# Twelve matmuls on zeros ahead of the first picks, a limit on the loads under way, and a new order, in a kernel of capped attention and a top-128 feed-forward block

## The chip, the core and the metric

The kernel runs on one core of a Trainium2 chip. A core has the engines TensorE (PE, matmuls), VectorE (DVE), ScalarE (ACT), GpSimd (POOL) and SyncE (SP, whose queue issues most of the transfers). The time of a run is the device time in microseconds. The kernel before was run three times.

## The reference

The first part is attention over 8 batches, 12 heads, 448 rows and a head width of 64. Scores are capped by a tanh before the softmax. The second part takes the 768 columns of all heads of a batch as one row per token, scores each token with a gate vector, picks the 128 best tokens of each batch, sends them through a feed-forward block of 768 to 1024 to 768 columns and adds the gated result to those tokens.

```python
scores = scale * np.matmul(q, k.transpose(0, 1, 3, 2))
scores = cap * np.tanh(scores / cap)
...
attn = attn / (np.sum(attn, axis=-1, keepdims=True) + 1e-09)
return np.matmul(attn, v).astype(np.float32)
...
    top_idx = np.argpartition(-scores[b], capacity)[:capacity]
    xe = x[b, top_idx]
    h = np.maximum(xe @ w1, 0.0)
    ye = h @ w2
    g = 1.0 / (1.0 + np.exp(-scores[b, top_idx]))
    out[b, top_idx] = x[b, top_idx] + g[:, None] * ye
```

## The kernel before, in words

**Tiling.** Four heads of a batch make a Double, so that there are 24 of them, three to a batch. Their keys are cut into three blocks of 128 rows and one of 64. The scores of a block of four heads are one unit for ScalarE: a tanh and then an exp over 128x1792 numbers. The 64-row blocks of two Doubles share a unit, so two Doubles make seven units, and the whole has 84. Scores are made on TensorE from q and k as they are (L691, "quarter" form) or from their splits into a high and a low part (`qh`, `ql`, `kh`, `kl`, made on VectorE at L647 and L653; L681, "wide" form). The values matmuls (L706) multiply the exponentials p of a block with v and accumulate in `psV`. When all four blocks of a Double are in, VectorE evacuates `psV` in two halves (L737, L738, L743 each); there is one `psV`, so the first values matmul of the next Double waits for the second half. A values step is 56 matmuls in a row of the trace, and a score unit is 16 in quarter form or 12 in wide form.

**Banks.** In the first phase the scores use six banks (`psE`, tanh and exp at L1252 and L1261). From unit `SIX` on they use four (`psS`, L1298 and L1305), and the two freed banks (`psT`) serve the picks and the feed-forward block.

**Feed-forward.** After the third Double of a batch VectorE has the gate scores of all its tokens (L772, L799, L801), sends them once through memory so that they lie in a row (L810, L813), counts for each token how many stand above it (L842, L850), and makes a one-hot matrix `sel` from the ranks (L881). TensorE's eight small "pick" matmuls (L891) turn it into the 128 indices, VectorE rounds them (L900 to L905), GpSimd gathers the rows (L909), TensorE transposes them (L938), and the two layers follow as 512- and 384-column matmuls (L992). Weights are split into high and low parts (L567, L570) as they arrive.

**What sets the order.** Every engine's instructions are written by a planner at build time, by a simulated clock for each engine. On TensorE the order of scores (Q) and values (V) steps is given by a string, `SCRIPT`; a number behind a letter says how many feed-forward pieces may go ahead of that step. For the other engines each task has a priority, which the table `EARLIER` shifts. The written order is what each engine executes; each instruction then only waits for its operands. SP issues all loads of q, k, v (L620) and weights (L555) and the stores of the results (L758, L761) from one queue, in order. A load waits until the buffer that it overwrites has been read.

## Time and profile before

| | |
|---|---|
| median of 3 runs | 435.36 us (434.31, 435.36, 437.21) |
| profiled execution | 435.0 us |
| its span | 433.2 us |
| TensorE matmul busy | 418.9 us, 97% of the span |
| ScalarE busy | 305.4 us, 71% |
| VectorE busy | 279.0 us, 64% |
| GpSimd busy | 27.5 us, 6% |
| granted TensorE clock, mean | 0.999 |
| chain that ended last | TensorE 81%, DMA 5%, ScalarE 5%, VectorE 3% |

The span is the time from the first to the last instruction of the profiled execution; 1.8 us of the execution lie around it. A time row reads: start and duration in microseconds, engine, line, operation, output and inputs, their shapes, and how many instructions the row joins; in brackets at the end how long the engine had stood idle before it, and what ended that. Ends of matmuls overlap the next start a little, so differences of starts are the better measure of their cost.

### The profile page before, as it was taken

To read this page: it belongs to the slowest core of one execution; us is meant where nothing else is said; L and a number is where in the kernel's file an instruction comes from. 1 tells how busy PE (TensorE), PEld (TensorE's weight loads), DVE (VectorE), ACT (ScalarE), POOL (GpSimd) and SP (SyncE) were. 2 spreads that over 40 slices of the span, in tenths; PEclk is the share of its full clock that TensorE was granted. 3 is DMA by queue.
4 is the path that set the end of the run, shared out by engine and by line. 5 is a ranking of instruction groups with operands and counts; after the bars stand their busy time and mean duration, and the time that the engine had idled before them with its cause. 6 is when DMAs were issued, how large, how long until landed. Compare 5 with 4: busy or idle time off the path is not lost.

```text
span 433.2 us, 17857 instructions
## 1 busy us (share of the span) xinstructions
PE 418.9 (97%) x8080; PEld 353.9 (82%) x8080; DVE 279.0 (64%) x861; ACT 305.4 (71%) x197; POOL 27.5 (6%) x73
## 2 busy tenths in 40 slices
PE   8989998999999999999999999999999999999994
PEld 5546586888799889898799888988789898879894
DVE  1596988959664688558745876738947695168241
ACT  5999999797886588694697586879787698411000
POOL 2000010100100001010010100101000010000101
PEclk9999999999999999999999999999999999999999
DMA  7995557550551562462181370472371321220202
GB/s 253 402 396 183 174 171 247 180 184 12 186 186 47 147 217 61 138 229 70 41 291 42 109 258 4 123 245 80 101 242 47 106 92 45 72 70 2 74 3 78
DMA packets 33268, 60.73 MB, mean 140 GB/s; under 512 B 10304, under 2 KB 20288, under 8 KB 33184
## 3 DMA queue, kind: packets, MB, share of 16 engines
q1 hardware_dynamic: 31456, 52.72, 37.1%
q0 software_dynamic: 1440, 6.56, 4.8%
q8 instruction: 65, 1.06, 1.0%
q10 hardware_dynamic: 288, 0.23, 0.2%
q14 instruction: 19, 0.16, 0.1%
HBM read 45.33 MB, written 14.17 MB: 137 GB/s over the span
## 4 chain that ended last, share of the span: by engine, by line
PE 81%; DMA 5%; ACT 5%; DVE 3%; issue 3%; POOL 1%; SPq 0%; POOLq 0%; DVEq 0%; ACTq 0%
PE psV L706 30%; PE psT L992 22%; PE psS L681 15%; PE psB L992 4%; PE psS L691 3%; DMA vlent<-in_v 2%; PE psE L691 2%; PE psE L681 2%; ACT p L1252 2%; ACT p L1261 1%; PE psT L938 1%; DMA p<-out,idx 1%; PE psV L992 1%; ACT plent L1261 1%; ACT plent L1252 1%
## 5 line engine op out<-in xcount | busy, mean ns | idle before, releaser
L706 PEld LDWEIGHTS psV<-v,p 128*64 128x64 f32 (+1 forms) x3864 | 104.8, 137 | 21.4 <-issue 14.7
L706 PE MATMUL psV<-v,p 128*64 128x65 f32 (+1 forms) x3864 | 111.6, 222 | 4.5 <-issue 2.4
L1298 ACT ACTIVATE p<-psS,sc 128x1792 f32<-128x1792 f32 x48 | 84.1, 1753 | 39.0 <-PE psS L681 22.7
L1305 ACT ACTIVATE p<-p,capc 128x1792 f32<-128x1792 f32 x48 | 86.1, 1794 | 1.4
L681 PE MATMUL psS<-qh,kh 64*128 64x448 f32 x220 | 42.6, 384 | 0.0
L706 PEld LDWEIGHTS psV<-v,plent 128*64 128x64 f32 (+1 forms) x1288 | 34.9, 137 | 8.1 <-issue 3.2
L737 DVE RECIPROCAL rec<-psV 128x7 f32<-128x7 f32 x48 | 9.6, 199 | 49.3 <-PE psV L706 49.3
L1298 ACT ACTIVATE plent<-psS,sc 128x1792 f32<-128x1792 f32 x16 | 28.0, 1752 | 16.9 <-PE psS L681 8.1
L706 PE MATMUL psV<-v,plent 128*64 128x65 f32 (+1 forms) x1288 | 37.6, 222 | 2.0 <-POOL vlent L667 1.2
L772 DVE CUSTOM_DVE_ANT_0 jk<-xn,gates 128x256 bf16<-128x256 f32 x72 | 30.4, 422 | 1.5
L1305 ACT ACTIVATE plent<-plent,capc 128x1792 f32<-128x1792 f32 x16 | 28.7, 1793 | 0.5
L738 DVE TENSOR_TENSOR xn<-psV,rec 128x384 f32<-128x384 f32 x48 | 26.8, 558 | 1.7
L1261 ACT ACTIVATE p<-p,capc 128x1792 f32<-128x1792 f32 x14 | 25.1, 1792 | 0.5
L1252 ACT ACTIVATE p<-psE,sc 128x1792 f32<-128x1792 f32 x14 | 24.3, 1737 | 0.6 <-PE psE L681 0.6
L842 DVE TENSOR_SCALAR_CACHE_REDUCE jk<-row,score 128x512 bf16<-128x512 f32 (+1 forms) x32 | 23.7, 742 | 0.9
L681 PEld LDWEIGHTS psS<-qh,kh 64*128 64x128 f32 x220 | 20.7, 185 | 2.6 <-ACT p L1298 0.2
L647 DVE CAST kh<-k 128x896 fp32r<-128x896 f32 x20 | 12.5, 624 | 13.0 <-PE psS L681 11.0
L992 PE MATMUL psT<-w2l,hh 64*128 64x384 f32 x192 | 20.7, 336 | 0.0
L681 PE MATMUL psS<-qlent,kh 64*128 64x448 f32 x112 | 20.5, 362 | 0.0
L681 PE MATMUL psS<-qh,klent 64*128 64x448 f32 x112 | 20.5, 362 | 0.0
L992 PE MATMUL psT<-w2h,hh 64*128 64x384 f32 x192 | 20.2, 339 | 0.0
L691 PE MATMUL psE<-q,k 64*64 64x448 f32 x176 | 19.6, 548 | 0.4 <-ACT p L1252 0.4
(179 smaller groups left out, 686.0 us busy)
## 6 DMA issues: line engine op xcount, KB each, us to landing
v<-in_v SPq DMA_DIRECT2D x23, 455.0 KB, 4.7
q<-in_q SPq DMA_DIRECT2D x22, 448.0 KB, 5.5
k<-in_k SPq DMA_DIRECT2D x22, 448.0 KB, 6.1
out<-xn SPq DMA_DIRECT2D x24, 384.0 KB, 4.7
stage<-in_moe_w SPq DMA_DIRECT2D x4, 512.0 KB, 7.9
stage<-in_moe_w SPq DMA_DIRECT2D x5, 384.0 KB, 4.3
row<-line SPq DMA_DIRECT2D x7, 256.0 KB, 3.9
out<-xt SPq DMA_DIRECT2D x48, 32.0 KB, 4.0
```

What stands on the lines that cost most here:

```text
L647: nc.vector.tensor_copy(t.slots[0].obj, self.at(nm))
L681: done += [tc.nc.tensor.matmul(banks[2 * r + j][:, :K.S], lhsT=a[HALF[j], r, c * P:(c + 1) * P], rhs=b[HALF[j], r, :], start=(n == 0), sto ...
L691: done += [tc.nc.tensor.matmul(banks[n][HALF[half], :K.S], lhsT=k[HALF[j], r, at:at + HD], rhs=q[HALF[j], r, :], start=True, stop=True).ins]
L706: tc.nc.tensor.matmul(D.acc.obj[HALF[g], r, i * WIDE:(i + 1) * WIDE], lhsT=p[rows, h, n * HD:(n + 1) * HD], rhs=v[rows, u, :], start=(c == ...
L738: nc.vector.tensor_tensor(slots[0].obj.rearrange("p c (r j d) -> p r j c d", r=2, j=2)[:, r], blocks[:, :2 * full, :K.D].rearrange("p (j c ...
L772: nc.vector.tensor_tensor_reduce(out=K.jk[:, :x.shape[1]], in0=x, in1=g, scale=1.0, scalar=0.0, op0=ALU.mult, op1=ALU.add, accum_out=part[ ...
L842: nc.vector.tensor_scalar(K.jk[:m], row[:m], score[:m, c:c + 1], None, op0=ALU.is_gt, op1=ALU.add, accum_out=rk.obj[:m, 0, c:c + 1])
L992: ins = nc.tensor.matmul(bank.obj[:, g, :width], lhsT=pair.obj[part][HALF[h], i, :], rhs=K.wts[r][HALF[h], i, g * width:(g + 1) * width], ...
L1252: a = nc.scalar.activation(slot.obj, K.S6[:, 2 * lo:2 * lo + 4, :K.S], AF.Tanh, scale=K.sc)
L1261: nc.scalar.activation(slot.obj, slot.obj, AF.Exp, scale=K.cap)
L1298: nc.scalar.activation(slot.obj, K.S4[:, :, :K.S], AF.Tanh, scale=K.sc)
L1305: nc.scalar.activation(slot.obj, slot.obj, AF.Exp, scale=K.cap)
```

## The change

- `SCRIPT` and `EARLIER` are replaced: most instructions of VectorE, and many steps of TensorE, stand elsewhere by a few places. `SIX` goes from 20 to 19, so the four-bank phase begins one unit earlier.
- `busy_work` lets the planner put matmuls on zeros (`idle_matmuls`) where it sees TensorE idle for at least 900 ns of its own clock and a free bank, up to 110 us. It does so at one place, with twelve.
- `in_flight` makes each load wait until the load four places before it has landed, and from the 41st load on the one two places before it. It holds for q, k, v, weights and the gate.
- The planner's own costs change (`stall`, the durations of steps, a wait of the scatters on the sweep before). They only move the order.
- `by_sides`, which would split `psV` in two, is switched off by a constant.

```diff
-SIX = 20
+SIX = 19
...
+LOADS, LATER_LOADS, EARLY = 4, 2, 40
+BY_SIDES = False
+DULL, KEEP, ONE, UNTIL = 900, 500, 58, 110000
...
-SCRIPT = ("Q Q Q1 V Q3 Q V Q4 Q24 V Q1 V2 Q6 Q9 V6 Q1 Q V12 Q Q38 Q V6 Q12 V Q Q15 Q V5 Q3 Q12 "
...
+def in_flight_limit(n):
+    return LOADS if n < EARLY else LATER_LOADS
+
+
+def in_flight(tc, K, ins):
+    if K.loose:
+        return
+    K.flight.append(ins)
+    n = in_flight_limit(len(K.flight) - 1)
+    if len(K.flight) > n:
+        tc.add_manual_dep(ins, K.flight[-n - 1].name,
+                          mybir.DependencyInfo(mybir.DependencyClass.Sync,
+                                               mybir.DependencyReason.DATA),
+                          reason="loads in flight")
...
-            tc.nc.sync.dma_start(s.obj, src[self.d])
+            in_flight(tc, K, tc.nc.sync.dma_start(s.obj, src[self.d]).ins)
...
+    def busy_work(self, task, start):
+
+        gap = start - self.clock["PE"]
+        free = self.banks.free
+        if gap < DULL or start >= UNTIL or not free or free[0].t > self.clock["PE"]:
+            return
+        n = int((gap - KEEP) / ONE)
+        self.stall(self.clock["PE"], ONE * n, 4 * n)
+        self.idle(task.shape, n)
...
+def idle_matmuls(tc, K, shape, n):
+
+    nc = tc.nc
+    zero = nc.const_aps.tensor(0.0, [P, P], F32)
+    bank = K.banks.slots[0].obj
+    for i in range(n):
+        a, b = HALF[i % 2], HALF[i // 2 % 2]
+        rows = slice(None) if shape == TALL else a
+        cols = slice(None) if shape == WIDTH else a if shape == TALL else b
+        nc.tensor.matmul(bank[cols, i % 2, :HD], lhsT=zero[rows, cols], rhs=zero[rows, :HD], start=True, stop=True)
```

TensorE, from the last values step of Double 4 to the first picks, before. `v_92` belongs to Double 4, `v_91` to Double 5; the picks are L891:

```order
L706 MATMUL psV<-v_92,p_94 64x65 x28
L681 MATMUL psE<-qh_107,kh_105 128x448 x2
...
L681 MATMUL psE<-qh_107,klent 128x448 x2
L706 MATMUL psV<-v_91,p_94 64x65 x28
L681 MATMUL psS<-qh_107,kh_105 128x448 x2
...
L681 MATMUL psS<-qh_107,klent 128x448 x2
L891 LDWEIGHTS sel_117
L891 MATMUL psT<-vals_71,sel_117 128x5
...
L706 MATMUL psV<-v_91,p_95 64x65 x28
```

The same place in the changed kernel, where L751 is the values step, L726 the scores, L1689 the zeros and L936 the picks:

```order
L751 MATMUL psV<-v_92,p_94 64x65 x28
L726 MATMUL psS<-qh_107,kh_105 128x448 x2
...
L726 MATMUL psS<-qh_107,klent 128x448 x2
L1689 MATMUL psT<-const-float32-0.0 128x64 x12
L936 LDWEIGHTS sel_117
L936 MATMUL psT<-vals_71,sel_117 128x5
...
L726 MATMUL psS<-qh_107,kh_105 128x448 x2
...
L751 MATMUL psV<-v_91,p_94 64x65 x28
```

The picks and one score step have moved ahead of the first values step of Double 5, and the zeros stand ahead of the picks; the score step in front of them is already in the four-bank phase.

VectorE at the same time, before, from the last count of the ranks to `sel`; L737, L738 and L743 are the two halves of the evacuation of Double 4:

```order
L647 CAST kh_104<-k_90 128x896
L842 TENSOR_SCALAR jk,rk_120<-row_112,score_118 64x512
L737 RECIPROCAL rec_102<-psV 128x7
L738 TENSOR_TENSOR xn_97<-psV,rec_102 128x2x3x64
L743 TENSOR_SCALAR xt_100<-psV,rec_102 128x64
L860 TENSOR_TENSOR rk_120<-rk_120 128x4
...
L737 RECIPROCAL rec_103<-psV 128x7
L738 TENSOR_TENSOR xn_97<-psV,rec_103 128x2x3x64
L743 TENSOR_SCALAR xt_100<-psV,rec_103 128x64
L881 TENSOR_SCALAR sel_117<-iota,rk_120 128x128 x4
```

The changed kernel (L692 the cast, L887 the count, L905 the ranks, L782 to L788 the evacuation, L926 `sel`):

```order
L887 TENSOR_SCALAR jk,rk_120<-row_112,score_118 64x512
L692 CAST kh_104<-k_90 128x896
L905 TENSOR_TENSOR rk_120<-rk_120 128x4
...
L782 RECIPROCAL rec_102<-psV 128x7
L783 TENSOR_TENSOR xn_97<-psV,rec_102 128x2x3x64
L788 TENSOR_SCALAR xt_100<-psV,rec_102 128x64
L926 TENSOR_SCALAR sel_117<-iota,rk_120 128x128 x4
L782 RECIPROCAL rec_103<-psV 128x7
L783 TENSOR_TENSOR xn_97<-psV,rec_103 128x2x3x64
L788 TENSOR_SCALAR xt_100<-psV,rec_103 128x64
```

`sel` has moved ahead of the second half of the evacuation, and the ranks ahead of the first.

SP's queue with what each transfer waits for, at the first burst of four loads behind the 41st load, before (`DMAHW` names the landing of an earlier transfer):

```order
L620 DMA q_87<-in_q 128x896 [waits DMAHW6_49,PE_49]
L620 DMA k_90<-in_k 128x896 [waits DMAHW7_49,DVE_49]
L620 DMA q_88<-in_q 128x896 [waits DVE_49]
L620 DMA k_89<-in_k 128x896 [waits DMAHW1_49]
L620 DMA v_91<-in_v 128x910 [waits DMAHW2_49,PE_49,Pool_49]
```

The changed kernel:

```order
L665 DMA k_90<-in_k 128x896 [waits DMAHW6_49,PE_49]
L665 DMA k_89<-in_k 128x896 [waits DMAHW2_49,DMAHW7_49,DVE_49,PE_49]
L665 DMA q_88<-in_q 128x896 [waits DMAHW6_49]
L665 DMA q_87<-in_q 128x896 [waits DMAHW7_49,DMAHW1_49,DVE_49]
L665 DMA v_91<-in_v 128x910 [waits DMAHW0_49,PE_49,Pool_49]
```

Both k now come ahead of both q, and q_88 waits for the landing of k_90, two loads before it.

## Rows read from the trace of the kernel before

**Rows 1.** The page's part 1, busy time, share and instructions of each engine.

```profile
PE   418.9 (97%) x8080; PEld 353.9 (82%) x8080; DVE 279.0 (64%) x861; ACT 305.4 (71%) x197; POOL 27.5 (6%) x73
```

**Rows 2.** Stretches: length, busy us of PE, PEld, DVE, ACT, POOL; clock, DMA share, GB/s.

```profile
10.00:20.00 10.00, 9.49 (x208) 6.20 (x205) 6.00 (x8) 9.90 (x6) 1.28 (x5) 1.00 0.99 396
70.00:77.50 7.50, 5.62 (x172) 4.71 (x168) 6.60 (x25) 6.68 (x4) 0.12 (x1) 1.00 0.60 200
77.50:87.00 9.50, 9.35 (x218) 7.74 (x214) 9.12 (x28) 7.32 (x6) 1.39 (x1) 1.00 0.61 193
200.00:300.00 100.00, 99.52 (x1952) 87.32 (x1950) 64.85 (x202) 76.35 (x49) 5.53 (x14) 1.00 0.42 132
```

**Rows 3.** Timeline of ACT, 74 to 85 us.

```profile
74.95 1.79 ACT L1261 ACTIVATE plent<-plent,capc 128x1792 f32<-128x1792 f32 x1
77.50 1.76 ACT L1298 ACTIVATE p<-psS,sc 128x1792 f32<-128x1792 f32 x1 [0.76 <-PE psS L681]
...
83.14 1.76 ACT L1298 ACTIVATE p<-psS,sc 128x1792 f32<-128x1792 f32 x1 [2.05 <-PE psS L691]
```

**Rows 4.** Timeline of PE, 72 to 87 us, around the first picks.

```profile
72.75 0.37 PE L681 MATMUL psE<-qh,klent 64*128 64x448 f32 x2
75.00 1.05 PE L706 MATMUL psV<-v,p 64*64 64x65 f32 x56 [1.88 <-issue]
75.98 0.47 PE L681 MATMUL psS<-qh,kh 64*128 64x448 f32 x2
...
77.31 0.26 PE L891 MATMUL psT<-vals,sel 64*128 64x5 bf16 x8
77.49 1.85 PE L706 MATMUL psV<-v,p 128*64 128x65 f32 x56
79.17 0.52 PE L706 MATMUL psV<-v,plent 128*64 128x65 f32 x12
...
82.98 0.59 PE L938 MATMUL psT<-ident,xe 64*128 64x64 f32 x12
...
86.61 1.56 PE L992 MATMUL psT<-w1h,xh 64*128 64x512 f32 x12
```

**Rows 5.** Timeline of DVE, 64 to 76 us, around the first `sel`.

```profile
64.92 0.28 DVE L817 TENSOR_TENSOR row<-row 128x64 f32<-128x64 f32 x1 [0.61 <-DMA row<-line]
...
71.07 0.63 DVE L647 CAST kh<-k 128x896 fp32r<-128x896 f32 x1 [0.56 <-DMA k<-in_k]
...
73.92 0.20 DVE L737 RECIPROCAL rec<-psV 128x7 f32<-128x7 f32 x1
...
74.82 0.73 DVE L881 TENSOR_SCALAR sel<-iota,rk 128x128 bf16<-128x128 bf16 x4
```

**Rows 6.** Timeline of PE elsewhere: form changes, and two stretches of later Doubles.

```profile
53.08 1.85 PE L706 MATMUL psV<-v,plent 128*64 128x65 f32 x56
54.86 0.47 PE L681 MATMUL psE<-qh,kh 64*128 64x448 f32 x2
...
109.18 1.85 PE L706 MATMUL psV<-v,p 128*64 128x65 f32 x56 [0.67 <-DVE xt L743]
...
131.52 0.36 PE L681 MATMUL psS<-qh,kh 64*128 64x448 f32 x2
```

**Rows 7.** Timeline of DVE, 119 to 129 us: one evacuation, and splits of k and q.

```profile
119.81 0.20 DVE L737 RECIPROCAL rec<-psV 128x7 f32<-128x7 f32 x1 [2.65 <-PE psV L706]
...
121.67 0.28 DVE L743 TENSOR_SCALAR xt<-psV,rec 128x64 f32<-128x64 f32 x1
...
125.34 0.63 DVE L647 CAST kh<-k 128x896 fp32r<-128x896 f32 x1 [1.79 <-PE psS L681]
...
127.74 1.09 DVE L653 TENSOR_TENSOR qlent<-q,qh 128x896 fp32r<-128x896 f32 x1
```

**Rows 8.** Timeline of SP's queue: last of four loads issued together.

```profile
115.74 0.43 SPq L620 DMA_DIRECT2D k<-in_k  x1
```

**Rows 9.** The page's part 6: issues, KB each, median us to landing.

```profile
k<-in_k SPq DMA_DIRECT2D x22, 448.0 KB, 6.1
```

More of the change, by code (lines that the diff above doesn't have):

```diff
@@ L280, in __init__ @@
         self.dma = 3700
+        self.count, self.edge, self.fetched = BEGUN, FIRST_EDGE, 0
+        self.loads = []
         self.policy = None
@@ L332, in finish @@
             if task.shape != self.shape:
-                busy += AFTER.get((self.shape, task.shape), 0)
+                busy += AFTER[task.shape] if self.shape is not None else 0
             self.shape = task.shape
+            busy += self.stall(start, busy, task.size)
         end = start + busy
@@ L353, in finish, with stall, ready @@
         self.wake()
+    def stall(self, start, busy, n):
+        add, count = 0, self.count
+        while n and self.edge <= count + n:
+            at = start + busy * ((self.edge - count) / n) + add
+            if self.fetched > at:
+                add += self.fetched - at
+                at = self.fetched
+            self.fetched = at + FETCH + SHARE * min(max(self.dma - at, 0), DEEP)
+            self.edge += CHUNK
+        self.count = count + n
+        return add
+    def ready(self, task):
+        r = task.ready()
+        if r is not None and task.kind in LOAD:
+            n = in_flight_limit(len(self.loads))
+            if len(self.loads) >= n:
+                r = max(r, self.loads[-n].t)
+        return r
     def candidate(self, e):
@@ L471, in allocate @@
     K.acc = Ring([bank(tc, K.stack, "V", [P, 2, 512])])
+    K.side = [Ring([None]) for _ in range(2)]
     K.banks = Ring([None])
@@ L700, in values_mm @@
     for i in range(K.NS):
-        for r in range(2):
+        for r in turns:
             for g in range(2):
@@ L999, in mm @@
                     tc.add_manual_dep(ins, gap[0].name, order, reason="rows change banks")
-        t = Task("PE", cost, mm, deps=[parts[i][part]] + (passed if m == last + 1 else []), take=[] if m else [K.banks],
+        t = Task("PE", cost, mm, size=4, deps=[parts[i][part]] + (passed if m == last + 1 else []), take=[] if m else [K.banks],
                  refs=[] if m else [2], reads=[pair] if m == 2 * last + 1 else [], prio=prio,
@@ L1087, in mm @@
                                  rhs=K.wts[r][:, i, cols], start=(m == 0), stop=(m == last))
-            t = Task("PE", 173, mm, deps=[parts[i][part]], take=[] if m else [K.banks],
+            t = Task("PE", 173, mm, size=2, deps=[parts[i][part]], take=[] if m else [K.banks],
                      refs=[] if m else [1], reads=[hp] if g and m == last else [], prio=(1, b),
@@ L1144, in begin @@
         acc.refs = 1
+        for r in K.side:
+            r.free.pop().refs = 1
         self.pair, self.half, self.S_free = [0, 0, None], 0, None
@@ L1164, in exp @@
             nc.scalar.activation(x, x, AF.Exp, scale=K.cap)
-        th = sim.add(Task("ACT", 1830, tanh, take=[K.p], refs=[1], reads=[acc], prio=0,
+        th = sim.add(Task("ACT", 1830, tanh, take=[K.p], refs=[1], prio=0,
+                          reads=[acc] + [r.slots[0] for r in K.side],
                           kind="tanh"))
@@ L1334, in value_est, with by_sides @@
         if c == D.units[0]:
[L1335 to L1339 removed]
+            for r in self.K.side[:1 if self.by_sides(D, c) else 2]:
+                a = r.next()
+                if a is None:
+                    return None
+                t = max(t, a.t + 50)
+        return t
+    def by_sides(self, D, c):
+        return BY_SIDES and c < self.K.NCH - 1 and c in (D.units[0], D.units[-1])
     def value_task(self):
@@ L1541, in fast_path @@
     sim = K.sim = FrontSim()
+    sim.banks, sim.idle = K.banks, lambda shape, n: idle_matmuls(tc, K, shape, n)
     plan(tc, K)
@@ L1683, in general_path @@
             values_mm(tc, K, D, c)
-        D.values.t = max(sim.clock.values())
+        D.accs = [[D.acc], [D.acc]]
+        for e in D.values:
+            e.t = max(sim.clock.values())
         sim.spawn(output_proc(tc, K, D))
```

386 lines of the change are left out of this document (204 added, 182 removed), and 44 rows, old and new, of tables (EARLIER, SCRIPT).

## The prediction, made before the run

> **What bounds the kernel now.** I read the page's shares first, then stretches of the span, then ScalarE's and TensorE's timelines around the first picks, since that is where the new matmuls stand. TensorE is busy for 418.9 of 433.2 us and no other engine for more than 71% [rows 1]. That mean hides two parts. In the first one ScalarE sets the pace: from 10 to 20 us it is busy for 9.90 of 10 us, and TensorE for 9.49 [rows 2]. ScalarE does a unit in 1.76 us of tanh and 1.79 us of exp [rows 3], and until 77 us hardly a gap stands between them; the first that counts are the 0.76 us at 77.50 and the 2.05 us at 83.14 [rows 3]. In the second part TensorE sets the pace: from 200 to 300 us it is busy for 99.52 of 100 us [rows 2]. What is taken from TensorE or given to it there is time; a wait in the first part is not, unless ScalarE runs dry for it.
>
> The place of the change lies between the two. TensorE's score step ends at 73.12 us (72.75 and 0.37); then it stands idle for 1.88 us until 75.00 [rows 4]. The trace has no releaser for that ("issue"), but the values step that starts then is the first of a Double and needs `psV` evacuated, and VectorE's second half of that work starts at 73.92 and has ended by 74.82, when `sel` follows [rows 5]. So this wait is one for the evacuation. Only then come scores (75.98) and the picks (77.31), the transposes of the gathered rows (82.98) and the first feed-forward matmul (86.61) [rows 4].
>
> **The change part by part.** The sum is made against the profiled execution, 435.0 us (span 433.2 and 1.8 around it), 0.36 us under the median of the three runs, 435.36.
>
> *The picks go ahead.* The work between 73.12 and 86.61 us is the same in both orders (scores, picks, three values steps of a full block and one of the tail, scores twice, transposes); only its order and the wait in it differ. In the new order the first thing that TensorE waits for is `sel`, not the evacuation. `sel` ran from 74.82 to about 75.5, behind both halves of the evacuation [rows 5]. One half, 0.90 us (73.92 to 74.82), now stands behind it, which makes it end at 74.6. The cast of k ahead of it waited 0.56 us for its load [rows 5]; that load is now the first of its burst, which can take up to 0.56 us off. The chain of counts began after 0.61 us of waiting for the row of scores [rows 5]; one weight subtraction now stands behind the scores, not before them, which can take off as much again. So `sel` ends between 73.4 and 74.6; I take 74.0, and the picks start 0.1 later. Then the picks (0.18), scores (1.33) and the tail's values step (0.98) [rows 4] follow without a wait, since the second half of the evacuation has ended by 74.9 and the values step gets to run at 75.6. They are through at 76.6; before, the same three were through at 77.49. **Gain 0.9 us**, between 0.3 (`sel` at 74.6) and 1.3 (`sel` early, and the zeros end last). ScalarE gets its next unit at about 75.6 and not after 77.31, and has no gap at 77.50; but TensorE sets the pace from there on, so I count nothing more for that.
>
> *The zeros.* The trace has no such matmul. Its nearest row is the twelve transposes of 64 columns, 0.59 us together [rows 4]; I take 0.6 us. From 73.1 to 73.7 they lie inside the wait for `sel` and cost nothing. At twice that price they would end at 74.3 and push the picks by 0.2. If `sel` came early enough that there were no wait, they would cost their whole 0.6.
>
> *Evacuation waits elsewhere.* At 109.18 us TensorE stands idle for 0.67 us until VectorE has evacuated [rows 6]. In the new order some 8 us of scores and feed-forward matmuls stand between the last values step of that Double and the next one's first: **gain 0.67 us**, certain but for the place that the freed work had. Two Doubles later in that stretch, and once more after 180 us, the reverse happens: 7 to 10 us of such work shrink to 2.45 by adding up the durations of its steps. An evacuation takes 2.14 us (119.81 to 121.67 and 0.28), two small instructions in between included [rows 7], so it just fits, unless another VectorE instruction of 0.6 to 1.1 us runs when the values step ends. **Cost 0.3 us** for both, between 0 and 1.6.
>
> *Changes of form.* Values followed by scores take 1.78 us from start to start (53.08 to 54.86) [rows 6], values followed by values 1.68 (77.49 to 79.17) [rows 4]: 0.10 us for each change of form. Counted through both orders there are 126 before and 121 now. **Gain 0.4 us**, between 0 (all in the first part, where ScalarE sets the pace) and 0.5.
>
> *Score steps closer together.* With four banks a score step can't start before ScalarE's tanh of the unit before is done, 1.76 us and some 0.1 at either end after the last scores. Adding up the steps of both orders, such a step comes 2.05 to 2.1 us after the last one at about 20 places now and at 7 before; the rest have more between them. Each of the 13 new places waits between nothing and 0.15 us. **Cost 0.5 us**, between 0 and 2.
>
> *The limit on loads* costs nothing in my sum. The first loads are needed by ScalarE's pace, and from 10 to 20 us the DMA engines were busy for 0.99 of the time at 396 GB/s [rows 2], so four large loads at a time should still fill them. Later the mean is 132 GB/s [rows 2]. The bounds are zero and the rival below. The tail after the last values step has almost the same order; I count 0, with 0.3 either way.
>
> The sum: 435.0 - 0.9 - 0.67 + 0.3 - 0.4 + 0.5 = 433.8 us. With all bounds on the good side it is 432.2, on the bad side 437.7 (435.0 - 0.3 - 0.67 + 1.6 + 2 + 0.3 less 0.2 for some changes of form).
>
> **The rivals.**
>
> *Nothing arrives.* The new order's gains are in waits, and waits move: the 0.9 us comes out again if the picks' result is not the next thing that anything needs, since TensorE had other values steps to do (it did until 82.98), and closer score steps eat the rest. For it: all of my terms are under 1 us. Against it: TensorE's idle time at 73.12 is real, and everything after it is dense. Time 435.0, between 434.4 and 436.
>
> *More than I see.* TensorE is idle for 14.3 of 433.2 us [rows 1]; some 6.5 lie at the start and end and can't go. If the new order closes half of the other 7.8 us, with the changes of form the time is 435.0 - 3.9 - 0.5 = 430.6. For it: the whole order is new. Against it: most of these waits lie before 77 us, where ScalarE would be in the way.
>
> *The limit of two makes later loads late*, the side of slower. Four loads of q and k were issued together, the last at 115.74 [rows 8], and land 6.1 us later at the median [rows 9]. With two at a time the second pair, both q, starts when the first has landed, at about 120.5, and lands at 126.6; a v load and the stores queue behind it on SP. The splits of k and q ran from 125.34 to 128.83 on VectorE [rows 7], q's from 127.1, and their first scores came at 131.52 [rows 6]. So there are 0.5 us before the split is held up and 2.7 more before the scores are. It decides if a pair takes more than about 7.7 us to land, or if the pair is itself issued 3 us late behind a store. Eight such bursts lie behind the 41st load; at 0.8 us each the time is 433.8 + 6.4 = 440.2. Against it: the loads have landed with 6.1 us as their median, early crowding included.
>
> *The clock makes the zeros matter.* The granted clock is 1.00 (2.4 GHz) in the stretch with the idle 1.88 us and in the next one [rows 2]. So that wait did not cost the clock in this execution and the zeros save nothing by it. If executions without a profile lost it there, work of 11.6 us (75.00 to 86.61 [rows 4]) would run at half the clock at worst; the spread of the three runs, 2.9 us, bounds it better. The kernel would then gain some 2 us besides the sum: 432.
>
> The Trainium skill, "TensorE: Matmul & The Clock Gate", section "Why this matters for your kernels", says that idle gaps between bursts of matmuls put the engine back to half its clock. By that rule the wait at 73 us is where the clock could go and the zeros would hold it; the trace does not bear it out for a gap of this size, since the clock stayed at 1.00.
>
> **How the numbers follow.** My forecast, 432.3 to 435 with 433.8 in the middle, gets 0.48; nothing arrives 0.20; more than I see 0.15; the late loads 0.11; the clock 0.06. About 1% is what a measurement of this kernel can tell from no change, so faster means under 431.0 us and slower over 439.7. Faster holds most of the third case and a little of the first: 0.15. Slower holds half of the late loads: 0.06. Within 1%: 0.79. The range goes from 430.8, which takes in part of the third case, to 437.4, about the sum with its bad bounds and the mild end of the late loads.
>
> **What would show it.** Right: the first picks start at 73.7 to 74.7 us with the zeros in the wait before them; the first feed-forward matmul starts about 0.9 us earlier than 86.61; ScalarE has no gaps of 0.76 and 2.05 us there; no evacuation wait near 109; the granted clock is 1.00 throughout. Wrong: a picks' start past 75.5; an idle TensorE that waits for VectorE's evacuation two Doubles later; score steps that wait for ScalarE by more than 2 us in all; casts of q that wait for a load, or scores that wait for these casts, at any burst after 110 us.

## The result: 1% slower, with the time lost in steps that the change does not touch

The changed kernel took 439.46 us, median of nine runs (438.49 to 441.22); the kernel before 435.36 (434.31 to 437.61, nine runs beside them). The ratio is 1.0085 with an interval of [1.0062, 1.0108]. The forecast was 433.8, with a range to 437.4, so both the sign and the range were wrong. The profiled execution has a span of 437.6 us, 4.4 more than the 433.2 of before. It answers to [rows 1] and [rows 2] with these lines (part 1 of the page, then the same four stretches):

```profile
PE 422.1 (96%) x8104; PEld 356.5 (81%) x8104; DVE 276.6 (63%) x859; ACT 306.5 (70%) x199; POOL 27.0 (6%) x73
```

```profile
10.00:20.00 10.00, 9.60 (x212) 6.68 (x216) 5.97 (x8) 9.90 (x7) 1.17 (x5) 1.00 1.01 381
70.00:77.50 7.50, 7.02 (x172) 6.33 (x170) 7.01 (x32) 7.16 (x5) 0.00 (x0) 1.00 0.69 242
77.50:87.00 9.50, 9.11 (x220) 6.74 (x218) 8.02 (x19) 7.81 (x7) 1.25 (x2) 1.00 0.60 170
200.00:300.00 100.00, 99.42 (x2016) 86.02 (x2013) 70.87 (x233) 79.48 (x52) 4.60 (x13) 1.00 0.46 138
```

The shares show almost nothing: TensorE looks as busy as before, and its clock is 1.00 in all four. The table of waits (who waited for whom: us in total, times, longest) points at the place. After, then before:

```profile
PE psV L751 <- issue: 4.0, 9, 1.2
PE psB L1037 <- DVE xh L762: 1.2, 1, 1.2
```

```profile
PE psV L706 <- issue: 2.6, 4, 1.9
PE psB L992 <- DVE xh L717: 0.7, 1, 0.7
PE psV L706 <- DVE xt L743: 0.7, 1, 0.7
```

The 1.9 us that the change was to take away are gone, and nine waits without a releaser ("issue") have taken the place of four, all of them on the line of the values steps. Four of them lie behind 190 us. These are their rows in TensorE's timeline, and below them GpSimd's indirect DMAs (line 1103, the scatters of finished batches) of the same moments. A row joins neighbouring steps and ends with the window that was asked for, so its count is not that of one step:

```profile
192.66 1.68 PE L751 MATMUL psV<-v,p 64*64 64x65 f32 x66
194.74 1.47 PE L751 MATMUL psV<-v,p 128*64 128x65 f32 x42 [0.41 <-issue]
...
256.68 0.46 PE L751 MATMUL psV<-v,p 64*64 64x65 f32 x11 [0.40 <-issue]
...
320.12 1.55 PE L751 MATMUL psV<-v,p 64*64 64x65 f32 x46 [0.34 <-issue]
...
361.31 0.89 PE L751 MATMUL psV<-v,p 64*64 64x65 f32 x19 [0.39 <-issue]
```

```profile
193.41 1.00 POOL L1103 DMA_INDIRECT out<-xe,idx  x1 [17.79 <-DMA v<-in_v]
255.38 1.25 POOL L1103 DMA_INDIRECT out<-xe,idx  x1 [4.00 <-DMA k<-in_k]
318.74 1.36 POOL L1103 DMA_INDIRECT out<-xe,idx  x1 [2.04 <-DMA out<-xt]
360.00 1.00 POOL L1103 DMA_INDIRECT out<-xe,idx  x1 [6.49 <-DVE xe L1098]
```

At each of the four a run of values matmuls is cut in two (I call this a cut). TensorE goes on 1.30 to 1.38 us after the scatter's start. Twice that is when the issue ends (255.38 and 1.25 is 256.63, TensorE resumes at 256.68; 318.74 and 1.36 is 320.10, it resumes at 320.12); behind the two issues of 1.00 us it is 0.3 us later. Nothing that the profile knows of was missing. Three cuts lie in a block of 64 rows, whose short matmuls follow each other fastest (56 matmuls and 56 weight loads in about 0.8 us). The first lies ten matmuls behind such a block, in the next full block. A gather at 78.56 (1.12 us) makes two shorter pauses, in the 64-row step behind the first picks and in the step after it.

To see what each place costs, I laid the executions beside each other by the work that TensorE had done (the sum of its steps' lengths, each form at one price) and read how much later each point was reached than before. `a_pad` is the experiment with eight idle memsets more on GpSimd, told below; no other engine's order differs between it and the changed kernel, and none of these pauses is in its profile.

```
us of work done    60    67.5   92.5   100    170    180    230    240    290    300    330    340    402
changed          +1.77  +2.36  +2.59  +1.81  +2.03  +2.57  +1.95  +2.72  +3.19  +4.17  +4.56  +5.38  +4.64
a_pad            +0.72  +0.45  +0.74  -0.02  +0.14  -0.17  -0.77  -0.89  -0.44  -0.27  +0.13  +0.16  -0.42
```

Between the two rows there are 1.05 us at work 60, then 0.86 (60 to 67.5, the gather), 0.85, 0.89, 0.81 and 0.79 (170 to 180, 230 to 240, 290 to 300, 330 to 340, the scatters), which is 4.2 us for the five; the rest of the 5.06 us at the end is -0.2. So a cut by a scatter shows 0.34 to 0.41 us of idle and costs about twice that: the matmuls just before it start more slowly too.

### The profile page after: what moved, and what is told of

Read it like the earlier page. It is cut to its first block, busy times and chain, and to the rows that moved or that the text cites. A ratio compares the mean times of both kernels' runs of the same rounds, so it can differ in the third digit from the quotient of the medians.

```text
span 437.6 us, 17906 instructions
## 1 busy us (share of the span) xinstructions
PE 422.1 (96%) x8104; PEld 356.5 (81%) x8104; DVE 276.6 (63%) x859; ACT 306.5 (70%) x199; POOL 27.0 (6%) x73
## 3 DMA queue, kind: packets, MB, share of 16 engines
q8 instruction: 65, 1.06, 1.0%
## 4 chain that ended last, share of the span: by engine, by line
PE 85%; ACT 7%; DMA 3%; DVE 2%; issue 2%; POOL 0%; POOLq 0%; DVEq 0%; ACTq 0%
PE psV L751 31%; PE psT L1037 24%; PE psS L726 17%; PE psB L1037 4%; PE psS L736 3%; ACT p L1306 2%; ACT p L1315 2%; PE psV L1037 2%; PE psT L983 1%; DMA k<-in_k 1%; PE psE L736 1%; PE psE L726 1%; PE psV L1677 1%; ACT plent L1315 1%; ACT plent L1306 1%
## 5 line engine op out<-in xcount | busy, mean ns | idle before, releaser
L751 PEld LDWEIGHTS psV<-v,p 128*64 128x64 f32 (+1 forms) x3864 | 105.8, 137 | 22.4 <-issue 17.0
L751 PE MATMUL psV<-v,p 128*64 128x65 f32 (+1 forms) x3864 | 113.3, 223 | 4.4 <-issue 3.6
L782 DVE RECIPROCAL rec<-psV 128x7 f32<-128x7 f32 x48 | 9.6, 199 | 63.1 <-PE psV L751 63.1
L726 PE MATMUL psS<-qh,kh 64*128 64x448 f32 x224 | 44.0, 388 | 0.5 <-ACT plent L1352 0.5
L751 PEld LDWEIGHTS psV<-v,plent 128*64 128x64 f32 (+1 forms) x1288 | 34.7, 137 | 6.7 <-issue 5.7
L1352 ACT ACTIVATE plent<-psS,sc 128x1792 f32<-128x1792 f32 x17 | 29.8, 1750 | 14.5 <-PE psS L736 7.7
L751 PE MATMUL psV<-v,plent 128*64 128x65 f32 (+1 forms) x1288 | 37.4, 222 | 0.4 <-issue 0.4
L1359 ACT ACTIVATE plent<-plent,capc 128x1792 f32<-128x1792 f32 x17 | 30.5, 1793 | 0.5
L726 PEld LDWEIGHTS psS<-qh,kh 64*128 64x128 f32 x224 | 21.2, 184 | 5.3 <-ACT plent L1352 1.6
L887 DVE TENSOR_SCALAR_CACHE_REDUCE jk<-row,score 128x512 bf16<-128x512 f32 (+1 forms) x32 | 23.7, 741 | 0.8
L726 PE MATMUL psS<-qh,klent 64*128 64x448 f32 x116 | 21.2, 362 | 0.0
L726 PE MATMUL psS<-qlent,kh 64*128 64x448 f32 x116 | 21.2, 362 | 0.0
L692 DVE CAST kh<-k 128x896 fp32r<-128x896 f32 x20 | 12.6, 631 | 12.1 <-PE psS L726 10.4
L1037 PE MATMUL psT<-w1h,xh 64*128 64x512 f32 x144 | 20.1, 401 | 0.0
```

Source lines behind the costliest of these rows:

```text
L692: nc.vector.tensor_copy(t.slots[0].obj, self.at(nm))
L726: done += [tc.nc.tensor.matmul(banks[2 * r + j][:, :K.S], lhsT=a[HALF[j], r, c * P:(c + 1) * P], rhs=b[HALF[j], r, :], start=(n == 0), sto ...
L751: tc.nc.tensor.matmul(D.acc.obj[HALF[g], r, i * WIDE:(i + 1) * WIDE], lhsT=p[rows, h, n * HD:(n + 1) * HD], rhs=v[rows, u, :], start=(c == ...
L887: nc.vector.tensor_scalar(K.jk[:m], row[:m], score[:m, c:c + 1], None, op0=ALU.is_gt, op1=ALU.add, accum_out=rk.obj[:m, 0, c:c + 1])
L1037: ins = nc.tensor.matmul(bank.obj[:, g, :width], lhsT=pair.obj[part][HALF[h], i, :], rhs=K.wts[r][HALF[h], i, g * width:(g + 1) * width], ...
L1352: nc.scalar.activation(slot.obj, K.S4[:, :, :K.S], AF.Tanh, scale=K.sc)
```

## The experiments

The record names the chip of each experiment: the first four ran on one chip, the others on three others. For the changed kernel itself and the kernel before beside it there is no name. This comes to matter.

**Is it the zeros, the limit or the order?** Three kernels take parts out of the changed one, with its order kept; one puts the limit into the kernel before.

```
a_nozero    - self.idle(task.shape, n)              (no matmuls on zeros)
a_nolimit   - if len(K.flight) > n:   + if False:   (no limit on loads)
a_neither   both of these
b_limit     + n = 4 if len(K.flight) <= 40 else 2   (kernel before, each load
            + tc.add_manual_dep(ins, K.flight[-n - 1].name, ...)    waits so)
```

> The changed kernel without its twelve matmuls on zeros; every other instruction, and the order, as in it. Zeros theory: the twelve take 1.28 us on TensorE in the trace of the changed kernel (74.52 to 75.80) and end after sel has (75.2 or before), so part of them is paid: 438.5 to 439, the picks start at about 75.2. Rival, the wait behind them: the scores after the picks wait for a tanh of ScalarE that ends at 76.47, zeros or not, so nothing is gained: 439.3 to 439.6. Order theory and limit theory: 439.3 to 439.6 too.

> The changed kernel without the waits of loads for earlier loads; the order of all engines' instructions is unchanged. Limit theory: weights land late in the first 60 us (VectorE waits 1.74 and 2.33 us for them at 48.30 and 54.72), and pairs of q and k late after that; without the limit the early waits of VectorE go and the time falls by 2 to 3 us, to 436.5 to 437.5. Order theory: the steps stand where TensorE waits for evacuations and for ScalarE, whatever the loads do; 439 to 439.5. Zeros theory: no difference.

> The changed kernel without the zeros and without the waits of loads for earlier loads: the new order alone. Limit theory: 436 to 437. Order theory: 438.5 to 439.5, nearly all of the loss is left. If both small causes add up to the whole loss: 435.4 or less.

> The kernel before with the limit on loads added (four under way, two from the 41st on) and its own order. Limit theory: slower by 1.5 to 3 us, 437 to 438.5, since its loads are in an order that was made without a limit. Order theory: 435 to 436, no difference.

Measured: `a_nozero` 438.66 us, ratio 1.0064 [1.0037, 1.0091]; `a_nolimit` 439.13, 1.0068 [1.0044, 1.0092]; `a_neither` 439.26, 1.0072 [1.0045, 1.0099]. All three are as slow as the changed kernel within their intervals, with the four cuts at the same places of the order. So neither zeros nor limit make the slowdown in this order, and taking 24 matmuls and 24 weight loads out of TensorE's stream ahead of the cuts doesn't move them.

Loads of instructions are in the trace, as DMA packets of the kind "instruction" (65 on the largest such queue, 1.06 MB). `a_nozero` has its last cut from 359.49 to 360.09 us, and from 357.50 to 360.20 no packet of any kind moves; `a_pad` has such a load in 355.40 to 356.60, beside a scatter over the same step, and no cut. First `a_nozero`, then `a_pad`:

```profile
DMA packets 0, 0.00 MB, mean 0 GB/s; under 512 B 0, under 2 KB 0, under 8 KB 0
```

```profile
q8 instruction: 1, 0.02, 6.5%
```

So neither a load of instructions nor any other transfer under way makes the cut. The Trainium skill, "Runtime: NRT & Kernel Launch", section "Instruction fetch mechanics", says that an engine's instructions are fetched in blocks of 16 KiB and that crossing a block is mostly hidden; these rows agree.

What the zeros do is seen in `a_neither`, which has none (TensorE's timeline, the picks):

```profile
73.66 0.67 PE L936 MATMUL psT<-vals,sel 64*128 64x5 bf16 x8 [0.59 <-DVE sel L926]
74.92 0.47 PE L726 MATMUL psS<-qh,kh 64*128 64x448 f32 x2 [0.59 <-ACT plent L1352]
```

and in the changed kernel:

```profile
74.52 1.45 PE L1689 MATMUL psT<-const-float32-0.0 64*128 64x64 f32 x24
75.80 0.24 PE L936 MATMUL psT<-vals,sel 64*128 64x5 bf16 x8
76.53 0.47 PE L726 MATMUL psS<-qh,kh 64*128 64x448 f32 x2 [0.48 <-ACT plent L1352]
```

The zeros take 1.28 us (74.52 to 75.80, 24 passes of 53 ns), not 0.6, and still cost nothing: without them TensorE waits 0.59 for `sel` and 0.59 for ScalarE instead.

They do bring something. Behind these two waits the granted clock of `a_neither` is 0.50 (1.2 GHz) for 3.4 us, in the changed kernel 1.00. The two stretches of `a_neither` (seventh number: granted clock), then the second one in the changed kernel:

```profile
73.00:76.50 3.50, 2.32 (x30) 1.59 (x32) 3.33 (x18) 3.47 (x3) 0.30 (x2) 1.00 0.40 131
76.50:79.90 3.40, 3.40 (x86) 3.28 (x84) 3.33 (x10) 3.40 (x4) 1.15 (x1) 0.50 0.80 213
```

```profile
76.50:79.90 3.40, 2.99 (x73) 2.21 (x74) 3.26 (x13) 3.39 (x3) 1.25 (x2) 1.00 0.47 140
```

`a_late_nozero`, told below, has the same fall (76.02 to 79.43), `a_nozero` with the same idle time has not, and none of the nine profiles of this order with zeros has one there. Over all executions, a mean clock of 0.995 or less came in 15 of 26 without the zeros and in 10 of 93 with them. In `a_late_nozero` the seven such executions have a median of 435.56 us, the other five of 433.90. The mean does not tell where a clock fell, and the medians of whole kernels do not show the gain.

`b_limit` took 441.68 us, 1.0124 [1.0094, 1.0154]: in the old order the limit does cost. The v load behind a burst goes out at 123.50, in the kernel before at 119.84. The rows are those of SP's queue, of GpSimd, of TensorE, and the stretches from 126 us on (seventh number: granted clock):

```profile
121.47 0.33 SPq L632 DMA_DIRECT2D k<-in_k  x1
123.50 0.33 SPq L632 DMA_DIRECT2D v<-in_v  x1
```

```profile
128.67 0.12 POOL L679 MEMSET v<- 128x14 f32 x1 [9.99 <-DMA v<-in_v]
128.76 0.09 POOL L987 MEMSET fence<- 1x1 f32 x1
```

```profile
128.90 2.93 PE L1004 MATMUL psT<-w2h,hh 64*128 64x384 f32 x16 [2.83 <-POOL fence L987]
131.76 1.80 PE L718 MATMUL psV<-v,p 64*64 64x65 f32 x56
```

```profile
126.00:129.00 3.00, 0.17 (x4) 0.10 (x2) 2.86 (x4) 2.85 (x2) 0.18 (x2) 0.87 0.63 215
129.00:131.00 2.00, 2.00 (x14) 2.00 (x16) 0.40 (x1) 0.70 (x1) 0.00 (x0) 0.50 0.03 8
...
133.00:135.00 2.00, 2.00 (x51) 1.88 (x46) 0.00 (x0) 0.00 (x0) 0.00 (x0) 0.50 0.03 8
135.00:137.00 2.00, 2.00 (x74) 2.00 (x72) 0.00 (x0) 0.00 (x0) 0.00 (x0) 0.99 0.00 0
```

GpSimd's memset of v waits for the load, a fence stands behind it, TensorE waits 2.83 us for the fence, and then the granted clock is 0.50 (1.2 GHz) for some 6 us: the 16 matmuls took 2.93 us, where the kernel before took 1.57 for them, the values step of 64 rows 1.80 and not 1.05. Together that one place costs 5.8 us by the time the clock is back. The Trainium skill, "TensorE: Matmul & The Clock Gate", section "Why this matters for your kernels", says that an idle gap between bursts drops the engine to half its clock. This gap bears it out. The wait of 1.88 us in [rows 4] does not, with a clock of 1.00 [rows 2]; but the same wait in `b_extra_tail`, told below, took 1.97 us and was followed by half the clock from 75.35 to 78.76.

**Is it the scatter's issue over a values step of 64 rows?** Two kernels take the scatters away from these steps; two lay extra gathers over such steps of the kernel before. `a_noscatter` leaves out the scatters of the first five batches; the extra gathers write into a buffer that nothing reads.

```
a_noscatter   + if b >= 5:                          (no scatter before that)
a_late        - deps=[end, (K.swept, SWEEP)]
              + deps=[(end, 3000), (K.swept, SWEEP)]   (3 us later in the plan)
              + tc.add_manual_dep(ins, K.mm[-1], ...)  (behind a values step)
b_extra_tail  + e = tc.nc.gpsimd.indirect_dma_start(out=K.extra[...], ...)  x13
              (released by the first matmul of that step)
b_extra_full  the same, by the first matmul of a full block's step
```

> The changed kernel without the scatters of the first five batches (their gated rows are not written); all else and its order as in it. GpSimd theory: while GpSimd issues an indirect transfer (1.0 to 1.4 us), TensorE gets its instructions more slowly, and a values step of a 64-row block, which takes them fastest, runs dry. In the changed kernel four scatters meet such a step (193.41, 255.38, 318.74 and 360.00 us), and TensorE stands idle 0.34 to 0.41 us within each and loses 0.74 to 0.96: without them 439.4 - 3.2 = 436.2. Rival, instruction fetch: the steps run dry at the edges of TensorE's instruction pages, scatters or not: 439.4. Rival, chance of position in the order: 439.4.

> The changed kernel with each scatter moved behind the values step that it met: it waits for the last values matmul that stands written 3 us after its own rows are ready. GpSimd theory: the scatters then meet full values steps, scores or feed-forward matmuls, which take instructions half as fast or slower; the idle times within the tail's values steps go, 436.2 to 436.8. Instruction fetch: 439.4. If the scatter's transfers as such disturb TensorE: the loss moves along with them, 439.4.

> The kernel before with thirteen additional indirect gathers of 128 rows of 64 bytes on GpSimd (from a weight into a tile of their own), each released by the first matmul of the values step of the 64-row block of Doubles 8 to 20. GpSimd theory: each costs 0.7 to 1.0 us, 435.4 + 9 to 13 = 444 to 448, with an idle time of TensorE in each of these steps. Rivals (fetch, transfers): the transfers are tiny, 435.4 to 436.5.

> The same thirteen gathers, released by the first matmul of the values step of the second 128-row block. GpSimd theory: such a step takes 112 instructions in 1.68 us, not in 0.82, and the scatters of the kernel before that met such steps left no gap over 0.17 us; 435.4 to 437. If any values step suffers alike: 444 to 448, as beside the 64-row steps. Rivals (fetch, transfers): 435.4 to 436.5.

Measured: `a_noscatter` 435.50 us, 0.9973 [0.9941, 1.0005]; `a_late` 434.90, 0.9984 [0.9957, 1.001]; the four cuts are gone in both. `b_extra_tail` 437.29, 1.0034 [1.0, 1.0069], but eleven of its thirteen gathers began only 0.55 to 0.60 us behind the step's start, over its second half; `b_extra_full` 435.53, 0.9993 [0.9964, 1.0022]. That the cuts went with the scatters looked like the proof. The next kernels took it away.

```
b_extra_early   as b_extra_tail, released by the ninth matmul ahead of the step
b_extra_big     the same with rows of 1536 bytes, not 64
a_late_nozero   a_late without the zeros
b_late          kernel before + deps=[(end, 3000)], + the wait of a_late
```

> The kernel before with the thirteen additional gathers of 128 rows of 64 bytes, released by the ninth matmul ahead of the values step of the 64-row block of Doubles 8 to 20 and not by its first, since released there they began 0.9 us late, when the step was nearly over. GpSimd theory, issue alone: each step that lies within an issue is idle until the issue ends, 0.4 to 0.9 us each, 435.4 + 5 to 11 = 440 to 447. If the transfer of long rows is needed for it, or the coupling needs a second condition: 435.5 to 438, with few or no idle times.

> The same with rows of 1536 bytes, 196 KB a gather, half of what a scatter of the kernel moves. GpSimd theory, issue alone: as with short rows, 440 to 447. If long rows are what disturbs: more than with short rows by 3 us or more. If neither: 435.5 to 438.

> The changed kernel with the late scatters and without the zeros. Zeros theory: another 0.5 to 1 us less than with the late scatters alone, 434. The wait behind them: the scores after the picks wait for ScalarE anyway, 434.9, no difference.

> The kernel before with its scatters moved in the same way. GpSimd theory: only one of its scatters met a tail's values step (191.22, idle 0.15, 0.44 us lost): 434.9 to 435.2, no difference that can be measured.

Measured: `b_extra_early` 435.61, 1.0003 [0.9982, 1.0024]; `b_extra_big` 436.03, 1.0026 [0.9998, 1.0054]; `a_late_nozero` 435.18, 0.9992 [0.9968, 1.0017]; `b_late` 435.14, 0.998 [0.995, 1.0009]. In the first two, eight and seven of the thirteen issues began between 0.50 us ahead of a values step of 64 rows and 0.12 behind its start, where the kernels with cuts have theirs too, and no step was cut. Not even the kernel's own scatter near 192 us was, which cuts its step in the kernel before. First `b_extra_early`, GpSimd and TensorE; then the kernel before, the same scatter and step:

```profile
193.53 1.37 POOL L1069 DMA_INDIRECT out<-xe,idx  x1 [3.73 <-DVE xe L1064]
```

```profile
193.85 2.33 PE L1559 MATMUL psV<-v,p 64*64 64x65 f32 x94
```

```profile
191.22 1.39 POOL L1058 DMA_INDIRECT out<-xe,idx  x1 [3.34 <-DVE xe L1053]
```

```profile
191.57 0.91 PE L706 MATMUL psV<-v,p 64*64 64x65 f32 x43
192.64 1.03 PE L706 MATMUL psV<-v,p 64*64 64x65 f32 x27 [0.15 <-issue]
```

The step starts 0.32 us behind the scatter in the one and 0.35 in the other. So an issue over such a step is not enough; something else has to be there. (The other cut of the kernel before, at 79.84 us behind the gather at 78.51, lies in a full block's step, so a 64-row block is not needed either.) All kernels without cuts had another GpSimd program, which made that the next theory.

**Does it take a certain GpSimd program?**

```
a_pad     + for _ in range(8): nc.gpsimd.memset(K.fence, 0.0)   (in the first us)
b_pad     the same in the kernel before
a_wait    + tc.add_manual_dep(ins, K.mm[-1], ...)   (a scatter also waits for the
                                                     last written values step)
```

> The changed kernel with eight memsets of one element more on GpSimd, all of them in the first microseconds; nothing else differs, and the order of the other engines' instructions is the same. If an issue of an indirect DMA starves TensorE whenever it lies over the values step of a 64-row block (lateness theory), nothing changes: the four idle stretches of 0.34 to 0.41 us inside such steps, near 194, 256, 320 and 361 us, stay, and the time is 438.5 to 440.5, ratio 1.006 to 1.011. If it takes besides that a certain place of GpSimd's instructions in its program (placement theory), as the kernels with another GpSimd program suggest, the idle stretches are gone or fewer, with at most two left, and the time is 435 to 437.5.

> The changed kernel with scatters that also wait for the matmul that ends the values step written last before them in the program, without the 3 us that were added where the scatters were moved; the places of the scatters in GpSimd's order stay, and by the order three of them get such a wait. Lateness theory: what counts is when a scatter is issued. One that gets pushed behind the values step of the 64-row block loses its idle stretch of 0.34 to 0.41 us; one that is still issued over such a step keeps it. With none pushed the time is 438.5 to 440.5, with one or two pushed 436.5 to 438.5. Placement theory: the waits alone change GpSimd's program, so that idle stretches go also where a scatter is issued over such a step as before; 434.5 to 437.

> The kernel before with the same eight memsets more on GpSimd. There one scatter, at 191.22 us, lies over a values step of a 64-row block and leaves TensorE idle for 0.15 us, and the gather at 78.51 does the same. Lateness theory: both stay, time 434.5 to 436.2, ratio 0.998 to 1.002. Placement theory: either they go, 434 to 435.5, or others come up at another of the eight scatters and gathers, each worth 0.3 to 1 us, up to 438.

Measured: `a_pad` 435.04 us, 0.9991 [0.9969, 1.0013], span 432.6; `a_wait` 434.62, 0.9977 [0.9953, 1.0001]; `b_pad` 435.14, 1.0008 [0.9988, 1.0029]. By these numbers eight memsets that do nothing would be worth 4.4 us. In `a_pad` the scatters meet the same steps at the same distances as in the changed kernel (0.76 us behind the step's start here, 0.75 there), and the steps stay whole; GpSimd, then TensorE:

```profile
191.53 1.01 POOL L1105 DMA_INDIRECT out<-xe,idx  x1 [17.80 <-DMA v<-in_v]
252.65 1.24 POOL L1105 DMA_INDIRECT out<-xe,idx  x1 [3.79 <-DMA k<-in_k]
```

```profile
190.77 2.83 PE L753 MATMUL psV<-v,p 64*64 64x65 f32 x112
...
252.49 1.05 PE L753 MATMUL psV<-v,p 64*64 64x65 f32 x56
```

**By the place of the scatter in that program?**

```
a_pad_mid   the eight memsets behind the third scatter, not at the start
a_pad1      one memset at the start
a_pad16     sixteen memsets at the start
```

> The changed kernel with the eight memsets behind the third scatter (255 us), not at the start. Placement theory: what counts is where a scatter's instructions lie in GpSimd's program, so only those behind the memsets change: the idle stretches near 194 and 257 us stay, those near 320 and 361 us go, and the time lies between, 436.3 to 438.3, ratio 1.002 to 1.006. If the eight memsets work in another way, by what they do to the first microseconds or to the whole program, either all four stay (438.5 to 440.5) or all four go (434.5 to 436).

> The changed kernel with a single memset more at the start. It tells how fine the placement is. If it counts by a few instructions, one memset moves or removes at least two of the four idle stretches (434.5 to 437.5); if it takes a larger shift, all four stay (438.5 to 440.5).

> The changed kernel with sixteen memsets more at the start. If only the one placement that the changed kernel happens to have is bad, the idle stretches are gone as with eight: 434.5 to 436.2. If good and bad placements alternate, some of the four or others come back, one at 0.7 to 1 us each: 436 to 440.

Measured: `a_pad_mid` 434.97 us, 0.9982 [0.9955, 1.0009]; `a_pad1` 435.16, 1.0003 [0.9982, 1.0025]; `a_pad16` 436.14, 1.003 [1.0002, 1.0057], without cuts as well. The first decides against the place: its scatter near 194 us stands ahead of the memsets, in a program that is the changed kernel's up to there, and its step is whole (GpSimd, TensorE):

```profile
194.73 1.01 POOL L1103 DMA_INDIRECT out<-xe,idx  x1 [17.80 <-DVE xe L1098]
```

```profile
193.98 2.83 PE L751 MATMUL psV<-v,p 64*64 64x65 f32 x112
```

**What stays open.** This list has, for each kernel, the pauses of over 0.3 us between the starts of two matmuls of values steps during the issue of an indirect DMA or just behind it (the wait for ScalarE near 246 us in the old order aside). The changed kernel and `a_nolimit` have two of them at one gather:

```
chip not named:    before 0.37 0.37             changed 0.37 0.46 0.63 0.61 0.56 0.61
the first four:    a_nozero 0.60 0.63 0.62 0.56 0.61     a_neither 0.60 0.62 0.57 0.60
                   a_nolimit 0.36 0.34 0.62 0.61 0.56 0.60     b_limit 0.31 0.35
all fourteen others, on three other chips:      none
```

These are 23 places with a cut. At every one TensorE goes on 1.27 to 1.41 us after the issue's start, while the issues themselves took 0.99 to 1.41. `a_neither` has no pause at its gather; that step fell into the half clock and ran at half the pace.

The fourteen without cuts differ from the six with cuts in two things at once: GpSimd's program, and the chip. In `a_pad_mid`, `a_late` and `a_noscatter` steps are whole that lie ahead of the first difference in GpSimd's program. So if it were the program, it would have to be something of the program as a whole, such as its length or where it lies in memory. Against that speaks `a_wait`. In its trace every engine has as many instructions as in the changed kernel, and GpSimd's 164 stand in the same order; only what three scatters wait for differs. Its fourth scatter is not one of the three, and it meets the same step in the same way (0.05 us ahead of its start in both). The step is whole, on another chip (GpSimd, TensorE):

```profile
314.92 1.35 POOL L1107 DMA_INDIRECT out<-xe,idx  x1 [1.99 <-DMA out<-xt]
```

```profile
314.97 4.67 PE L751 MATMUL psV<-v,p 64*64 64x65 f32 x168
```

So the chip is the better reading: every kernel on the chip of the first four has cuts, none on the three others. The kernel before, which ran beside all of them, settles nothing. Its median is highest on the chip of the first four, 436.20 (17 runs), against 435.69, 435.53, 435.28 and 435.09 beside the others (35, 35, 25 and 25 runs); its two cuts cost 0.41 and 0.49 us beside `b_pad`; but the first and the last of these four are from one chip and differ by 0.60, and the median beside the changed kernel itself was 435.36, with both cuts in its profile. The chip is argued, not shown: the run that would show it, the changed kernel itself on one of the other chips, was not made. Why an issue holds TensorE up at all stays open too.

No kernel is clearly faster than the kernel before.

## Why the prediction was wrong

**The step that failed is one that was not in the sum.** I went through what TensorE waits for, and counted the moved steps of TensorE, VectorE and ScalarE; where GpSimd's scatters and gathers come to lie against TensorE's steps in the new order had no term, and "nothing" was its unspoken price. The trace of before had the row for it: a values step cut at 192.64 us by 0.15 us of "issue", shown above, with a scatter over it. Two meetings with a cut in the old order, five in the new one: 4.2 us less 0.9 is 3.3 of the 4.1 us between the medians. The other part, 1.05 us, is the more that the changed execution lost in the first 71 us than `a_pad` did; in the twelve profiles of this order TensorE starts the step at that place anywhere from 70.00 to 73.58 us (71.78 in the changed kernel), so I don't count it as the change's. What was missing is a term for these meetings. The price that the row shows would not have held on every chip: on three others they cost nothing. Without cuts, eight kernels of this order took 434.62 to 436.14 us, inside the range of the forecast.

**The picks.** Forecast: `sel` done at 74.0, picks from 74.1, and then everything without a wait, a gain of 0.9. VectorE's and ScalarE's rows after:

```profile
72.28 0.61 DVE L692 CAST kh<-k 128x896 fp32r<-128x896 f32 x1
...
74.46 0.73 DVE L926 TENSOR_SCALAR sel<-iota,rk 128x128 bf16<-128x128 bf16 x4
```

```profile
74.72 1.75 ACT L1352 ACTIVATE plent<-psS,sc 128x1792 f32<-128x1792 f32 x1 [0.27 <-PE psS L726]
```

The cast of k no longer waits for its load, as forecast; `sel` still started only 0.36 us earlier than before (74.46, not 74.82 [rows 5]). The picks came at 75.80, past the 75.5 that I had named as the sign of failure, and the scores behind them then waited 0.48 us for a tanh that began at 74.72. I had stated that rule myself (with four banks a score step can't start before the tanh of the unit before is done) and applied it everywhere but here. In `a_neither`, which was not late, the picks start at 73.66, somewhat ahead of where I had put them, and the same wait takes 0.59. So of the 0.9 us nothing arrived: `a_pad` gained 0.27 us between work 60 and 67.5, and the cut that the old order has there and `a_pad` has not is worth 0.31. The first feed-forward matmul, forecast 0.9 us ahead of 86.61, came at 88.61, and at 86.70 in `a_pad`. This is the "nothing arrives" rival in small: the picks' result was not what TensorE needed next. One reading of mine was loose as well: ScalarE had stood idle for 0.63 us at 55.77 already; no term hangs on it.

**The zeros** were priced at half (0.6, measured 1.28), and cost nothing, though for the reason above and not because `sel` was late. That they hold the clock I had only as a rival.

**The evacuation at 109 us.** Forecast a gain of 0.67; it came: between work 92.5 and 100 the lag shrinks by 0.78 us (2.59 to 1.81). The values step stands there without a wait, where [rows 6] had 0.67:

```profile
109.75 1.45 PE L751 MATMUL psV<-v,p 128*64 128x65 f32 x42
```

**Covers at later Doubles, score steps, changes of form, tail.** I gave them +0.3, +0.5, -0.4 and 0. No cover fell short: no values step behind the picks waits for VectorE. A feed-forward step waits 0.47 us for it instead, which no term had. Score steps waited for ScalarE nowhere behind the picks. The changes of form no run prices by itself. The tail's wait for VectorE grew from 0.72 to 1.17 us, past my 0.3:

```profile
347.59 1.65 PE L1037 MATMUL psT<-w2h,hh 64*128 64x384 f32 x16 [0.47 <-DVE rec L782]
...
387.31 0.73 PE L1037 MATMUL psB<-w1h,xh 64*128 64x512 f32 x4 [1.17 <-DVE xh L762]
```

**The sum without the cuts.** `a_pad` has the changed order, limit and zeros and no cuts, `b_pad` the old order and no cuts, and both ran on the same chip: 435.04 and 435.14 us, spans of 432.6 and 432.7. So of what I did count, 1.2 us of gain, the medians show 0.1, near the "nothing arrives" rival at 435.0. They can't exclude the 1.2: the interval of `a_pad` alone reaches from 1.35 us of gain to 0.57 of loss, and the eight kernels of this order without cuts have a mean ratio of 0.9992, some 0.4 us of gain. The traces say where it went: 0.67 gained at 109 us, 0.48 gained where the old order waits for ScalarE, 0.47 and 0.45 given back at the feed-forward step and in the tail. The row of the old order:

```profile
246.10 1.85 PE L706 MATMUL psV<-v,p 128*64 128x65 f32 x56 [0.48 <-ACT p L1305]
```

**The limit.** Its rival's number, 440.2, is close to the result, by chance: with the changed order the limit costs nothing that `a_nolimit` could show. That the danger is real `b_limit` showed, in the old order, in another way than mine: not the casts of q, but a v load whose memset holds a fence on GpSimd's queue. I had named that v load as queued behind the pair, and not asked who waits for it.

**The clock** stayed at 1.00 there in the profiled executions of both kernels, so this rival does not describe the result. Its mechanism is real all the same: in the old order one of eight profiles, `b_extra_tail`, loses the clock behind this wait and 1.5 us with it, and without the zeros two of three do. I had given it 0.06 and a gain of 2 us; a gain of a size like that comes only in the executions that would have lost the clock.

## What to carry to other kernels

A gap in the middle of a run of equal matmuls that has no releaser is a price like any other: look at which other engine is issuing something at that moment, and count how often the new order lays the two over each other. Before 1% is put down to an order, run the unchanged candidate on a second chip: here eight idle memsets seemed to be worth more than the whole change, and one missing control leaves the chip argued and not shown. Matmuls that only fill a wait should be judged by the clock of many executions, since one profile may keep its clock without them. And a result brought forward pays only if the step behind it can run: follow the next two steps, each with its own engine and buffer, before the gain is written down.

## What the runs showed that I had not expected

- Around GpSimd's issue of an indirect DMA (0.99 to 1.41 us), TensorE stood idle inside runs of values matmuls, for 0.34 to 0.41 us in most places and as little as 0.09 in others, in six kernels, and went on 1.27 to 1.41 us after the issue's start; where the cost was measured it was 0.4 to 0.9 us a meeting. In fourteen kernels on three other chips such meetings left no trace.
- Twelve matmuls on zeros over 64 columns were 24 passes of 53 ns, 1.28 us, about twice the twelve transposes of 64 columns (0.59 us [rows 4]).
- An idle TensorE of 2.83 us was followed by some 6 us at half the clock, one of 1.97 us by 3.4 us; one of 1.88 us was not [rows 2, 4]. Two waits of 0.59 us with only the picks between them were followed by 3.4 us at half the clock, and twelve matmuls on zeros in their place kept it at 1.00.
